# First rows of tile 0 loaded in two transfers and multiplied in four pieces, the last wide store issued by ScalarE, and a new plan of the whole order

## The chip, the cores and the metric

The kernel runs on one core of a Trainium2 chip. The metric is the time of one execution on the device in microseconds (us). Five engines work side by side, each through its own queue in order: TensorE (PE; its weight loads are listed as PEld), VectorE (DVE), ScalarE (ACT), GpSimd (POOL) and SyncE (SP), which issues the DMA transfers. They wait for each other on semaphores.

## What is computed

```python
# x: (2, 4160, 192), weight_gen: (2, 4160, 8 heads, 7)
w = softmax(weight_gen, axis=-1)
a[b, s, h] = sum_k w[b, s, h, k] * x_pad[b, s + k, h]          # 7 rows back, 24 columns a head
xk, xr = mu_k * a + (1 - mu_k) * a_prev, mu_r * a + (1 - mu_r) * a_prev
v = sigmoid(xr @ w_r) * (relu(xk @ w_k) ** 2 @ w_v)            # 192 -> 1024 -> 192
h = relu(v @ w_in)                                              # 192 -> 1024
out = (h * sigmoid(conv3(h, conv_w))) @ w_out                   # 1024 -> 192
```

All data are float32. A float32 product is split on the chip into a high and a low part, so that each product is several TensorE passes; the weights are split in the same way, once, at the start.

## The kernel before

The sequence of each batch is cut into ten tiles, `SIZES` = 238, 238, seven of 476, and 352 columns. For a tile i and a batch b the kernel loads rows of x (`rows`), multiplies them by the softmax weights `sw` into `prod` (seven products of 192 columns for a token slot), and sums the seven (`tok`). For tile 0 and for the slots named in `SUMS` TensorE adds them with an identity matrix and ScalarE copies the sum out; for all other slots GpSimd makes three additions. `mixing` turns tokens into columns and makes `xA` and `xB`. The first network (`moe1`: banks `pa`, sums in the banks `am` and `ar`, its split activations in `s`) and the second (`moe2`: banks `pc`, activations `h` and `g`, sums in the banks `bm` and `br`) each run over eight chunks of 128 of the 1024 columns. `store` empties `bm` and `br` and writes 128 wide and 64 narrow output rows (wide from `om` or `stage`, narrow from `att`).

In the first 70 us the weights come in too. `prepare` loads them through a ring of three buffers in `stage` and splits each chunk on ScalarE, VectorE and TensorE, with `bm` and `br` as places of work; in the names below `stage<-bm`, `pc<-stage` and `g<-stage,pc` are three VectorE steps of such a chunk. Twenty-six warming matmuls (`WARM`) that use only `signs` stand ahead of the real work on TensorE.

The order is not the one in which the code is written. Every operation is recorded with a wished time; `Program.schedule` then plans. A forward walk keeps a time for each engine, starts the ready operation of highest rank, and holds back two operations that share the SBUF port (`shares`: any GpSimd operation, and a VectorE operation with two operands in SBUF). A backward walk gives new ranks. After `ROUNDS` of the two, the operations are issued by their planned start (line 255, which is why every line of the profile says L255). `PACE` stretches the cost of every operation on an engine, `SLACK` is added where TensorE waits for that engine, and 3.507 us are added to each transfer. So a new number in these tables moves operations over the whole program, and the order that each engine executes is fixed when the kernel is built.

`attention` (line 569) holds `load` and `token`, `store` (line 971) holds `e0`, `e1` and `e2`.

Of the kernel before, what the change touches and what calls it, by code (L numbers as in the profile page):

```python
# [12 lines left out]
ALU = mybir.AluOpType  # L13
AX = mybir.AxisListType

NB, SEQ, DM, NH, KS, DFF = 2, 4160, 192, 8, 7, 1024
# [8 lines left out]
PART = [128] * NTILE  # L25
SLOTS = [2, 2] + [4] * 7 + [3]
EXTRA = [0] + [p * l - n for p, l, n in zip(PART, SLOTS, SIZES)][1:]
PAD = KS - 1
# [1 line left out]
NF = DFF // 128  # L30
LAG = 12
WARM = 26
SLACK = {"ACT": 0.311, "DVE": 0.274, "POOL": 0.239}
PACE = {"ACT": 1.045, "DVE": 1.035, "POOL": 1.037}
ROUNDS = 13
HELD = [85.0, 140.0, 215.0, 290.0, 365.0, 440.0, 515.0]
HIGH = range(5)
LOWS = {(NTILE - 1, NB - 1, k) for k in range(6, NF)}
SUMS = {(1, 0, 1), (1, 1, 0), (1, 1, 1)}
MODES = [0, 0, 0, 0, 0, 0, 2, 2, 2, 2, 2, 0, 2, 2, 2, 2, 2]  # L40

S_LAG, G_LAG = 3.25, 4.75
# [11 lines left out]
class Program:  # L54
# [81 lines left out]
    def schedule(self):  # L136
        n = len(self.ops)
# [46 lines left out]
        hold = ready  # L184
# [23 lines left out]
        def forward(rank):  # L208
            nonlocal when
            when = hold[:]  # L210
            start, last, table = [0.0] * n, 0.0, ACTF.Exp
            wires = dict.fromkeys(self.real, 0.0)

            def step(i, eng, t):
                nonlocal last, table
                start[i] = t
                if turns[i] is not None:
                    t = t + (0.0 if turns[i] == table else 1.3)
                    table = turns[i]
                end = t + late[i]  # L220
                if load[i]:
                    wires[eng] = max(wires[eng], t + dur[i] + 0.55) + moved[i]
                    end = wires[eng] + 3.507
                last = max(last, end)
                for j in succ[i]:
                    when[j] = max(when[j], t + dur[i] if eng in ("PE", "POOL") and eng == name[j] else end + slack(i, name[j]))
                return t

            walk((pred, succ), lambda i: (rank[i], i), step)
            return start, last  # L230

        def backward(start, last):
            nonlocal when
            full = [dur[i] + 0.55 + moved[i] + 3.507 if load[i] else late[i] for i in range(n)]
            when = [full[i] - dur[i] for i in range(n)]
            rank = [0.0] * n

# [32 lines left out]
def conv_moe_kernel(ctx: ExitStack, tc: tile.TileContext, xp, wg_first, wg_rest, w_k, w_v, w_r, w_in, conv_w, w_out, out):  # L270
# [116 lines left out]
    def at(t, fn, hold=0.0):  # L387
        plan.append((t, len(plan), fn, hold))
# [180 lines left out]
    def attention(i, b, t_load, t, dt_, eng, hold=(0.0, 0.0)):  # L569
        L = SLOTS[i]  # L570

        def load():
            rows_t[i, b] = rows_r()[:, :L + PAD]
            row = b * (SEQ + PAD) + STARTS[i] - EXTRA[i]
            SP.dma_start(out=rows_t[i, b], in_=bass.AP(tensor=xp.tensor, offset=xp.offset + row * DM, ap=[[L * DM, PART[i]], [1, (L + PAD) * DM]]))

        def token(l):
            if i not in tok_t:
                tok_t[i] = tok_r()
            p = prod_r()  # L580
            y = p.rearrange("p (k d) -> p k d", k=KS)
            w = sw[:, sum(slots[:i]) + b * L + l].unsqueeze(2).to_broadcast([128, KS, DM // NH, NH])
            eng.tensor_tensor(p.rearrange("p (k g h) -> p k g h", k=KS, h=NH),
                              rows_t[i, b][:, l:l + KS].rearrange("p k (g h) -> p k g h", h=NH), w, op=ALU.mult)
            if i < 1 or (i, b, l) in SUMS:

                def total():
# [17 lines left out]
            eng.tensor_tensor(tok_t[i][:, l, b * DM:b * DM + DM], y[:, 0], y[:, 1], op=ALU.add)  # L605

        at(t_load, load, hold[0])
        for l in range(L):
            at(t + l * dt_, lambda l=l: token(l), hold[1])

# [360 lines left out]
    def store(i, b, t):  # L971
# [11 lines left out]
        def e1():  # L983
            st["m"] = omt_r()
            ACT.activation(st["m"][:, :n], acc2["m"][:, :n], ACTF.Copy, scale=0.5)
            SP.dma_start(out=out[b, 0:128, t0 + a:t0 + n], in_=st["m"][:, a:n])

        def e2():
            DVE.scalar_tensor_tensor(out=st["b"][:, :n], in0=acc2["r"][0:64, :n], scalar=0.5, in1=st["b"][:, :n], op0=ALU.mult, op1=ALU.add)
# [158 lines left out]
```

## Time and profile before

| | us |
|---|---|
| median of 3 runs | 696.65 (696.64 to 696.85) |
| the profiled execution | 697.28 |
| span of its instructions, first to last | 695.5 |

| engine | busy us | share of the span | instructions |
|---|---|---|---|
| PE | 684.3 | 98% | 3473 |
| PEld | 603.6 | 87% | 3473 |
| ACT | 630.1 | 91% | 1333 |
| DVE | 589.9 | 85% | 1003 |
| POOL | 531.3 | 76% | 388 |

Matmuls are pipelined: a drawn matmul of 476 columns is 0.38 us long while the next one starts after some 0.22 us. So short stops of TensorE vanish in these pictures, and only what is longer than the overlap is shown as idle. A row of the timeline gives start, duration, engine, line, operation, output and input, the number of equal instructions merged, and in brackets the idle time of the engine before it with what ended it.

### The profile page before, as it was taken

The page shows a single profiled execution, that of the slowest core. Times are in us where ns is not written, and L with a number is a line of the kernel's source. Part 1 is how long each engine was busy: PE and PEld are TensorE (multiplying, and loading weights), DVE is VectorE, ACT ScalarE, POOL GpSimd, SP SyncE. Part 2 cuts the span into 40 slices and gives each one's busy share as a digit, 9 for nine tenths or more (in the row PEclk, how much of TensorE's full clock was granted, in tenths as well). Part 3 has the DMA queues.
Part 4 walks back from the last instruction along what each step waited for, and adds up shares of the span by engine and source line. Part 5 has one row for each costly group of instructions (what it writes and reads, how often), then busy time and mean ns, then how long its engine had stood idle before and what let it go on. Part 6 is the DMA issues. An engine that isn't in the chain of part 4 may idle for free.

```text
span 695.5 us, 10541 instructions
## 1 busy us (share of the span) xinstructions
PE 684.3 (98%) x3473; PEld 603.6 (87%) x3473; DVE 589.9 (85%) x1003; ACT 630.1 (91%) x1333; POOL 531.3 (76%) x388
## 2 busy tenths in 40 slices
PE   8999999999999999999999999999999999999997
PEld 7799887888888888888888888888888888899997
DVE  7999998889879898988798978988897768686787
ACT  4988899999999998999999899898999999999996
POOL 3899999996998699669976997599929996243335
PEclk9999999999999999999999999999999999999999
DMA  8987021222022321130222112121202000200011
GB/s 290 267 210 238 24 68 42 68 89 63 8 86 64 86 51 42 64 85 12 77 68 66 28 57 93 32 56 57 80 22 70 8 28 14 65 8 28 6 33 31
DMA packets 20791, 48.43 MB, mean 70 GB/s; under 512 B 3457, under 2 KB 16257, under 8 KB 20609
## 3 DMA queue, kind: packets, MB, share of 16 engines
q1 hardware_dynamic: 20736, 47.77, 23.6%
q8 instruction: 27, 0.44, 0.3%
q14 instruction: 28, 0.22, 0.1%
HBM read 27.40 MB, written 6.39 MB: 49 GB/s over the span
## 4 chain that ended last, share of the span: by engine, by line
PE 87%; DVE 6%; ACT 3%; DMA 2%; issue 1%; SPq 0%; DVEq 0%
PE pa L255 25%; PE pc L255 21%; PE bm L255 13%; PE am L255 12%; PE br L255 8%; PE ar L255 7%; DVE pc L255 2%; DMA wkB<-x 1%; DMA sw<-in_rest_dram 1%; DVE s L255 1%; ACT pc L255 1%; DVE g L255 1%; ACT pa L255 1%; DVE stage L255 1%; DVE mk L255 0%
## 5 line engine op out<-in xcount | busy, mean ns | idle before, releaser
L255 POOL TENSOR_TENSOR prod<-rows,sw 128x1344 f32<-128x1344 f32 x68 | 210.3, 3093 | 14.4 <-PE pa L255 11.6
L255 DVE SCALAR_TENSOR_TENSOR pc<-h,cw,pc 128x476 f32<-128x476 f32 (+1 forms) x276 | 193.6, 704 | 27.2 <-ACT pc L255 24.5
L255 ACT ACTIVATE pa<-pa 128x476 f32<-128x476 f32 (+2 forms) x280 | 151.9, 547 | 11.7 <-PE pa L255 9.2
L255 POOL TENSOR_TENSOR prod<-prod 128x576 f32<-128x576 f32 (+1 forms) x126 | 154.3, 1225 | 8.4
L255 PE MATMUL bm<-g,wo 128*128 128x476 f32 (+1 forms) x411 | 135.3, 376 | 0.4 <-ACT stage L255 0.4
L255 PE MATMUL am<-s,wv 128*128 128x476 f32 (+2 forms) x464 | 129.8, 357 | 0.0
L255 PE MATMUL pa<-xA,wkA 128*128 128x476 f32 (+2 forms) x438 | 112.0, 360 | 0.8 <-DVE s L255 0.8
L255 PE MATMUL pc<-x,wiA 128*128 128x478 f32 (+1 forms) x414 | 111.7, 375 | 0.4 <-ACT x L255 0.2
L255 DVE TENSOR_TENSOR s<-pa,s 128x476 fp32r<-128x476 f32 (+1 forms) x137 | 86.6, 633 | 19.5 <-ACT s L255 18.7
L255 PE MATMUL br<-g,wo 128*128 128x476 f32 (+1 forms) x274 | 100.6, 375 | 0.0
L255 PE MATMUL ar<-s,wv 128*128 128x476 f32 (+2 forms) x336 | 99.8, 350 | 0.0
L255 ACT ACTIVATE h<-pc 128x478 f32<-128x478 f32 (+1 forms) x138 | 78.3, 568 | 17.9 <-PE pc L255 16.6
L255 ACT ACTIVATE pc<-h,cw 128x476 f32<-128x476 f32 (+1 forms) x138 | 91.7, 665 | 0.8
L255 ACT ACTIVATE pc<-pc 128x476 f32<-128x476 f32 (+1 forms) x152 | 84.3, 555 | 8.3 <-DVE pc L255 4.5
L255 POOL TENSOR_TENSOR g<-stage,g 128x476 fp32r<-128x476 f32 (+1 forms) x41 | 47.5, 1160 | 56.0 <-ACT g L255 44.1
L255 PEld LDWEIGHTS pa<-xA,wkA 128*128 128x128 f32 x438 | 79.0, 188 | 12.2 <-DVE s L255 1.3
L255 PEld LDWEIGHTS am<-s,wv 128*128 128x128 f32 x464 | 81.0, 188 | 9.3
L255 PEld LDWEIGHTS pc<-x,wiA 128*128 128x128 f32 x414 | 76.3, 188 | 11.7 <-DVE g L255 1.0
L255 PEld LDWEIGHTS bm<-g,wo 128*128 128x128 f32 x411 | 76.5, 188 | 11.1 <-ACT stage L255 0.8
L255 PE MATMUL pa<-xB,wkB 128*128 128x476 f32 (+2 forms) x292 | 82.7, 359 | 0.0
L255 PE MATMUL pc<-x,wiB 128*128 128x478 f32 (+1 forms) x276 | 81.7, 376 | 0.0
L255 ACT CAST s<-pa 128x476 fp32r<-128x476 f32 (+1 forms) x137 | 76.4, 558 | 1.1
(170 smaller groups left out, 1178.2 us busy)
## 6 DMA issues: line engine op xcount, KB each, us to landing
rows<-in_x_dram SPq DMA_DIRECT2D x14, 960.0 KB, 5.0
xB<-rm SPq DMA_DIRECT2D x28, 119.0 KB, 2.3
rows<-in_x_dram SPq DMA_DIRECT2D x4, 768.0 KB, 6.6
xB<-mk SPq DMA_DIRECT2D x16, 119.0 KB, 2.3
rows<-in_x_dram SPq DMA_DIRECT2D x2, 864.0 KB, 5.3
r<-r SPq DMA_DIRECT2D x14, 119.0 KB, 2.2
x<-x SPq DMA_DIRECT2D x14, 119.0 KB, 2.2
out_dram<-stage SPq DMA_DIRECT2D x7, 238.0 KB, 2.0
```

Source lines behind the costliest of these rows:

```text
L255: getattr(self.real[eng], method)(*a, **k)
```

## The change

Four things are edited. The load of tile 0, batch 0 becomes two transfers of four rows each, at their place in one queue. Its two products become four instructions: first those of the rows of the first transfer (part 0), then those of the second (part 1). The last wide store is issued from ScalarE's queue, right behind the activation that fills `om`, no longer from SP's. And the plan is made with other numbers: `PACE`, `SLACK`, `ROUNDS`, 2.668 us for a transfer's end, and another set `SUMS` (slot 1 of tile 1, batch 0 now goes through GpSimd's additions, slot 3 of tile 2, batch 0 through TensorE).

```diff
-SLACK = {"ACT": 0.311, "DVE": 0.274, "POOL": 0.239}
-PACE = {"ACT": 1.045, "DVE": 1.035, "POOL": 1.037}
-ROUNDS = 13
+SLACK = {"ACT": 0.101, "DVE": 0.164, "POOL": 0.427}
+PACE = {"ACT": 1.038, "DVE": 1.018, "POOL": 1.022}
+ROUNDS = 16
...
-SUMS = {(1, 0, 1), (1, 1, 0), (1, 1, 1)}
+SUMS = {(1, 1, 0), (1, 1, 1), (2, 0, 3)}
...
-                    end = wires[eng] + 3.507
+                    end = wires[eng] + 2.668
...
-            SP.dma_start(out=rows_t[i, b], in_=bass.AP(tensor=xp.tensor, offset=xp.offset + row * DM, ap=[[L * DM, PART[i]], [1, (L + PAD) * DM]]))
+            for p, q in ((0, 4), (4, L + PAD)) if (i, b) == (0, 0) else ((0, L + PAD),):
+                SP.dma_start(out=rows_t[i, b][:, p:q], in_=bass.AP(tensor=xp.tensor, offset=xp.offset + (row + p) * DM,
+                                                                   ap=[[L * DM, PART[i]], [1, (q - p) * DM]]))
...
-        def token(l):
+        def token(l, part=None):
...
+            k0, k1 = (0, KS) if part is None else ((0, 4 - l), (4 - l, KS))[part]
...
+            eng.tensor_tensor(y[:, k0:k1].rearrange("p k (g h) -> p k g h", h=NH),
+                              rows_t[i, b][:, l + k0:l + k1].rearrange("p k (g h) -> p k g h", h=NH), w, op=ALU.mult)
+            if part == 0:
+                return
...
+        if (i, b) == (0, 0):
+            for part in range(2):
+                for l in range(L):
+                    at(t + (2 * part + l) * 0.03, lambda l=l, part=part: token(l, part), hold[1])
+            return
...
-            SP.dma_start(out=out[b, 0:128, t0 + a:t0 + n], in_=st["m"][:, a:n])
+            (ACT if last and b == 1 else SP).dma_start(out=out[b, 0:128, t0 + a:t0 + n], in_=st["m"][:, a:n])
```

VectorE at the head of the program, from the products of tile 0 on, before the change (`sw` are the softmax weights, `am` its place of work, `prod_82` and `prod_83` the products of the two slots):

```order
L255 TENSOR_TENSOR prod_82<-rows_80,sw 128x1344
L255 TENSOR_TENSOR prod_83<-rows_80,sw 128x1344
L255 TENSOR_SCALAR stage<-bm 128x512
L255 TENSOR_SCALAR pc_114<-stage 128x512
L255 TENSOR_REDUCE am<-sw 128x32
L255 SCALAR_TENSOR_TENSOR g_76<-stage,pc_114 128x512
L255 TENSOR_SCALAR stage<-br 128x512
L255 TENSOR_TENSOR sw<-sw,am 128x224
```

The same stretch of VectorE's queue after the change:

```order
L255 TENSOR_TENSOR prod_82<-rows_80,sw 128x768
L255 TENSOR_TENSOR prod_82<-rows_80,sw 128x576
L255 TENSOR_SCALAR stage<-bm 128x512
L255 TENSOR_TENSOR prod_83<-rows_80,sw 128x576
L255 TENSOR_SCALAR pc_114<-stage 128x512
L255 TENSOR_TENSOR prod_83<-rows_80,sw 128x768
L255 SCALAR_TENSOR_TENSOR g_76<-stage,pc_114 128x512
L255 TENSOR_SCALAR stage<-br 128x512
L255 TENSOR_REDUCE am<-sw 128x32
L255 TENSOR_SCALAR pc_114<-stage 128x512
```

The chunk's steps now stand between the pieces of the products, and `g_76` and `stage<-br` stand ahead of the reduction `am<-sw`, behind which `g_76` stood before.

VectorE where tile 0's result `x2_0` is written and tile 2 is mixed (`stage<-stage,pa1` and `att0`), at 72 us of the profile, before:

```order
L255 TENSOR_TENSOR wo_70<-pc0_114,g2_78 128x2x64
L255 SCALAR_TENSOR_TENSOR x2_0_73<-am_116,x2_0_73 128x238
L255 SCALAR_TENSOR_TENSOR x2_0_73<-am_116,x2_0_73 64x238
L255 TENSOR_TENSOR s0_104<-pc1_115,s0_104 128x476
L255 TENSOR_TENSOR stage_75<-stage_75,pa1_113 128x476
L255 SCALAR_TENSOR_TENSOR stage_75<-stage_75,onemu_61,pa1_113 128x476 x2
L255 SCALAR_TENSOR_TENSOR pc0_114<-h0_108,cw_62,pc0_114 128x476 x2
L255 TENSOR_TENSOR s1_105<-pa0_112,s1_105 128x476
```

The same place after:

```order
L255 TENSOR_TENSOR wo_70<-pc0_114,g2_78 128x2x64
L255 TENSOR_TENSOR stage_75<-stage_75,pa1_113 128x476
L255 SCALAR_TENSOR_TENSOR x2_0_73<-am_116,x2_0_73 128x238
L255 SCALAR_TENSOR_TENSOR x2_0_73<-am_116,x2_0_73 64x238
L255 SCALAR_TENSOR_TENSOR stage_75<-stage_75,onemu_61,pa1_113 128x476 x2
L255 TENSOR_TENSOR s0_104<-pc1_115,s0_104 128x476
L255 SCALAR_TENSOR_TENSOR pc0_114<-h0_108,cw_62,pc0_114 128x476 x2
L255 TENSOR_TENSOR att0_86<-att0_86,pa1_113 64x476
L255 TENSOR_TENSOR s1_105<-pa0_112,s1_105 128x476
```

One step of the mixing now stands ahead of `x2_0`, and another (`att0`) ahead of `s1`.

TensorE where the first unit's sums in `bm` are finished (the last `bm<-g3`) and the next unit's begin (`bm<-g0`), at 113 to 117 us of the profile, before:

```order
L255 MATMUL bm_118<-g3_79,wo_70 128x476 x3
L255 MATMUL br_119<-g3_79,wo_70 128x476
L255 MATMUL am_116<-s3_107,wv_69 128x476
L255 MATMUL pa1_113<-xA00_92,wkA_65 128x476 x3
L255 MATMUL pa1_113<-xB01_97,wkB_66 128x476 x2
L255 MATMUL br_119<-g3_79,wo_70 128x476
L255 MATMUL ar_117<-s3_107,wv_69 128x476
L255 MATMUL bm_118<-g0_76,wo_70 128x476 x2
```

The same place after, from the last `bm<-g3` on:

```order
L255 MATMUL bm_118<-g3_79,wo_70 128x476
L255 MATMUL am_116<-s0_104,wv_69 128x476
L255 MATMUL pa0_112<-xA10_94,wrA_71 128x476 x3
L255 MATMUL pc0_114<-x2_1_74,wiA_67 128x478 x3
L255 MATMUL pc0_114<-x2_1_74,wiB_68 128x478 x2
L255 MATMUL pa0_112<-xB11_100,wrB_72 128x476 x2
L255 MATMUL am_116<-s0_104,wv_69 128x476
L255 MATMUL ar_117<-s0_104,wv_69 128x476
```

Before, nine matmuls stood between the last use of `bm` and its next; now there are 31 (the next `bm<-g0` comes 22 rows below the first row shown).

## Rows read from the trace of the kernel before

**Rows 1.** Windows: length, then busy us (instructions) of PE, PEld, DVE, ACT, POOL; clock.
```profile
10.00:80.00 70.00, 65.97 (x467) 59.59 (x466) 65.97 (x143) 59.63 (x154) 62.69 (x41) 1.00 0.73 210
80.00:120.00 40.00, 39.43 (x203) 33.16 (x202) 36.70 (x59) 37.38 (x78) 38.00 (x27) 1.00 0.18 54
120.00:680.00 560.00, 560.00 (x2701) 492.57 (x2701) 470.13 (x769) 520.63 (x1077) 422.56 (x306) 1.00 0.18 50
```
**Rows 2.** Timeline of PE in the dense stretch: start us, duration us.
```profile
140.35 0.81 PE L255 MATMUL pa<-xA,wkA 128*128 128x476 f32 x3
140.99 0.60 PE L255 MATMUL pa<-xB,wkB 128*128 128x476 f32 x2
```
**Rows 3.** Timeline of all engines at the end of the program.
```profile
690.99 0.47 PE L255 MATMUL bm<-s,wo 128*128 128x354 f32 x2
...
691.68 0.52 DVE L255 SCALAR_TENSOR_TENSOR att<-br,att 64x353 f32<-64x353 f32 x1 [1.17 <-ACT att L255]
692.17 0.34 SPq L255 DMA_DIRECT2D out_dram<-om  x1
692.60 0.49 SPq L255 DMA_DIRECT2D out_dram<-att  x1
```
**Rows 4.** Timeline of PE at the head.
```profile
7.01 0.88 PE L1080 MATMUL ar<-signs 128*128 128x256 f32 x6
7.74 3.16 PE L255 MATMUL pa<-prod,ident 128*128 128x192 f32 x18
...
12.81 0.50 PE L255 MATMUL bm<-g,signs 128*128 128x512 f32 x1 [0.72 <-DVE g L255]
```
**Rows 5.** Timeline of DVE at the head.
```profile
6.03 3.03 DVE L255 TENSOR_TENSOR prod<-rows,sw 128x1344 f32<-128x1344 f32 x2
8.98 0.68 DVE L255 TENSOR_SCALAR stage<-bm 128x512 uint32<-128x512 uint32 x1
9.70 0.69 DVE L255 TENSOR_SCALAR pc<-stage 128x512 uint32<-128x512 uint32 x1
11.59 0.57 DVE L255 TENSOR_REDUCE am<-sw 128x32 f32<-128x224 f32 x1 [1.20 <-DMA sw<-in_rest_dram]
12.07 0.68 DVE L255 SCALAR_TENSOR_TENSOR g<-stage,pc 128x512 fp32r<-128x512 uint32 x1
...
13.27 0.38 DVE L255 TENSOR_TENSOR sw<-sw,am 128x224 f32<-128x224 f32 x1
13.56 0.69 DVE L255 TENSOR_SCALAR pc<-stage 128x512 uint32<-128x512 uint32 x1
...
14.89 0.56 DVE L255 TENSOR_REDUCE am<-sw 128x32 f32<-128x224 f32 x1
```
**Rows 6.** Timeline of SP at the first load of rows.
```profile
1.19 0.42 SPq L255 DMA_DIRECT2D rows<-in_x_dram  x1
```
**Rows 7.** DMA issues of that moment: KB each, us to landing.
```profile
rows<-in_x_dram SPq DMA_DIRECT2D x1, 768.0 KB, 4.6
```
**Rows 8.** Timeline of ACT at the first chunk of weights.
```profile
7.54 0.64 ACT L255 ACTIVATE bm<-stage 128x512 f32<-128x512 f32 x1 [3.20 <-DMA stage<-in_moe_w_k_dram]
```
**Rows 9.** Timeline of DVE from 72 us on.
```profile
72.73 0.84 DVE L255 SCALAR_TENSOR_TENSOR x<-am,x 128x238 fp32r<-128x238 f32 x2 [0.55 <-ACT x L255]
73.60 0.66 DVE L255 TENSOR_TENSOR s<-pc,s 128x476 fp32r<-128x476 f32 x1
74.17 0.64 DVE L255 TENSOR_TENSOR stage<-stage,pa 128x476 f32<-128x476 f32 x1
```
**Rows 10.** Timeline of PE from 77 us on.
```profile
78.17 0.60 PE L255 MATMUL pa<-xA,wkA 128*128 128x238 f32 x3 [0.80 <-DVE s L255]
```
**Rows 11.** Timeline of PE from 115.5 us on.
```profile
116.49 0.69 PE L255 MATMUL bm<-g,wo 128*128 128x476 f32 x2 [0.36 <-ACT stage L255]
```
**Rows 12.** Waits of PEld from 80 to 120 us: total, times, longest.
```profile
PEld pc L255 <- DVE g L255: 1.0, 2, 0.5
```
**Rows 13.** Timeline of POOL from 10 us on.
```profile
10.34 3.04 POOL L255 TENSOR_TENSOR prod<-rows,sw 128x1344 f32<-128x1344 f32 x1 [8.99 <-PE pa L255]
```

More of the change, by code (lines that the diff above doesn't have):

```diff
@@ L233, in backward @@
             nonlocal when
-            full = [dur[i] + 0.55 + moved[i] + 3.507 if load[i] else late[i] for i in range(n)]
+            full = [dur[i] + 0.55 + moved[i] + 2.668 if load[i] else late[i] for i in range(n)]
             when = [full[i] - dur[i] for i in range(n)]
@@ L574, in load @@
             row = b * (SEQ + PAD) + STARTS[i] - EXTRA[i]
-            SP.dma_start(out=rows_t[i, b], in_=bass.AP(tensor=xp.tensor, offset=xp.offset + row * DM, ap=[[L * DM, PART[i]], [1, (L + PAD) * DM]]))
-        def token(l):
+            for p, q in ((0, 4), (4, L + PAD)) if (i, b) == (0, 0) else ((0, L + PAD),):
+                SP.dma_start(out=rows_t[i, b][:, p:q], in_=bass.AP(tensor=xp.tensor, offset=xp.offset + (row + p) * DM,
+                                                                   ap=[[L * DM, PART[i]], [1, (q - p) * DM]]))
+        prod = {}
+        def token(l, part=None):
             if i not in tok_t:
                 tok_t[i] = tok_r()
-            p = prod_r()
+            if part != 1:
+                prod[l] = prod_r()
+            p = prod[l]
+            k0, k1 = (0, KS) if part is None else ((0, 4 - l), (4 - l, KS))[part]
             y = p.rearrange("p (k d) -> p k d", k=KS)
-            w = sw[:, sum(slots[:i]) + b * L + l].unsqueeze(2).to_broadcast([128, KS, DM // NH, NH])
-            eng.tensor_tensor(p.rearrange("p (k g h) -> p k g h", k=KS, h=NH),
-                              rows_t[i, b][:, l:l + KS].rearrange("p k (g h) -> p k g h", h=NH), w, op=ALU.mult)
+            w = sw[:, sum(slots[:i]) + b * L + l, k0:k1].unsqueeze(2).to_broadcast([128, k1 - k0, DM // NH, NH])
+            eng.tensor_tensor(y[:, k0:k1].rearrange("p k (g h) -> p k g h", h=NH),
+                              rows_t[i, b][:, l + k0:l + k1].rearrange("p k (g h) -> p k g h", h=NH), w, op=ALU.mult)
+            if part == 0:
+                return
             if i < 1 or (i, b, l) in SUMS:
```

## The prediction

> **What bounds the kernel now.** I read the windows first, since an average over the program mixes a loaded head with a dense body. From 120 to 680 us TensorE (PE) is busy in 560.00 of 560 us, at a granted clock of 1.00 [rows 1]; the other engines are not. In that stretch a matmul of 476 columns starts every (140.99 − 140.35)/3 = 0.213 us [rows 2]. The change leaves the number of TensorE's products as it is (one slot of `SUMS` is swapped for another), so no plan can shorten those 560 us. What can be won is what PE loses ahead of 120 us and what lies outside its work: 4.03 us of drawn idle time from 10 to 80 us and 0.57 us from 80 to 120 us [rows 1], some 4.6 us together, then the 7.74 us before its first product [rows 4], and the tail after its last [rows 3]. The drawn idle time is too small a count: three matmuls drawn as one take 0.81 us, so one is drawn as 0.81 − 2 x 0.213 = 0.38 us, and each stop hides 0.38 − 0.21, some 0.16 us more.
>
> Second, who makes PE wait there. VectorE (DVE) is busy in 65.97 of the 70 us from 10 to 80 us, idle for as long as PE is, and the stops that I opened name its results [rows 4, 10, 12]. So up to about 80 us the time is set by a chain in which DVE is nearly always full: a step taken off DVE, or an idle hole of DVE filled, moves PE. ScalarE (ACT) with 59.63 us and GpSimd (POOL) with 62.69 us of 70 have more room [rows 1]. Third, the rows at the two ends.
>
> The sum is made against the profiled execution, 697.28 us (695.5 of span and 1.78 around it); the median, 696.65, lies 0.63 us below it.
>
> **The tail.** DVE fills `att` from 691.68 to 692.20, SP issues the store of `om` at 692.17 for 0.34 us, and only at 692.60 that of `att`, with 0.49 us [rows 3]. With `om` issued from ACT's queue, SP is free and takes `att` at about 692.22: 0.38 us earlier. ACT has nothing behind that issue. No ACT issue of a transfer is in this trace. If it costs 0.49 us, as the longer of the two in [rows 3], `om` is on its way at 692.66, still ahead of the 693.09 that `att` needed; if it starts later than SP's by as much as the gain, 0.38 us, nothing is left, and by more it is a loss. Bounds −0.38 and +0.2, I take **−0.38**, since the issue stands right behind ACT's own activation and needs no signal to another engine.
>
> **The start of PE.** The first rows now come as 2 x 384 KB. I expect no gain from that alone. The load is issued at 1.19 us and takes 4.6 us to land, 5.8 us [rows 6, 7], while DVE begins the products at 6.03 us [rows 5] and PE's warming matmuls, ahead of the first product in its queue, last until 7.74 us [rows 4]. The one extra issue on SP costs 0.42 us [rows 6]; the transfers behind it are limited by what is queued in the DMA engines by then, so it costs nothing as long as a backlog stands; without that cover the second chunk and all behind come 0.42 us later.
>
> **The head on DVE.** A product of 1344 elements takes 3.03/2 = 1.515 us; `sw<-sw,am`, of the same form with 224, 13.56 − 13.27 = 0.29 us. That makes 1.225/1120 = 1.094 ns an element and 0.045 us for an instruction, so 0.885 us for a piece of 768 and 0.675 us for one of 576, and the four 3.12 us, 0.09 us more than now [rows 5]. The other half of the rows lies behind the first 512 KB chunk of `w_k` in the queue, with the same bytes ahead of it as that chunk had, so it lands when that did, about 7.5 us [rows 8], and the chunk lands earlier by the time of 384 KB: 512 KB took 7.5 − 5.8 = 1.7 us, so 384 KB 1.3 us, and ACT's first step on it starts near 6.2 us. DVE then: piece to 6.92, wait to 7.55, piece to 8.23, `stage` (9.70 − 8.98 = 0.72 us) to 8.95, piece to 9.62, `pc` 0.72 us to 10.34, last piece to 11.23, and `g` starts at 11.23 us where it started at 12.07 [rows 5]. PE's stop before 12.81 [rows 4] ends some 0.85 us earlier. But the reduction that stood ahead of `g` now comes later: from `g` to the second reduction DVE took 14.89 − 12.07 = 2.82 us, and 12.07 − 11.59 = 0.48 us for the first, so it gets there at 11.23 + 3.30 = 14.53, not 14.89: −0.36 us [rows 5]. Bounds −0.36 (the whole is kept) and +0.1 (the 0.09 of the split, nothing kept); I take **−0.25**, as the second chunk, which DVE needs behind `g`, lands no earlier than before.
>
> **From there to 78 us.** At 72.73 DVE stood idle for 0.55 us, waiting for ACT's `x`, and a mixing step `stage<-stage,pa` followed [rows 9]. In the new order this step stands ahead of `x2_0` and fills the hole: −0.55. But `att0` now stands ahead of `s1`, and a step of 476 columns of this kind takes 74.17 − 73.60 = 0.57 us [rows 9]; PE waited for that `s` at 78.17 with 0.80 us of idle time [rows 10]. So −0.55 + 0.57 = +0.02, and with the head **−0.23** up to 78 us.
>
> **From 78 to 120 us.** The 0.57 us of `att0` are no more to be done. PE's weight loads stood still twice for DVE's `g`, 1.0 us together [rows 12]. Bounds 0 (the step has only moved inside a queue that stays full) and −1.0; I take half, **−0.5**, near the 0.57 us of the step. At 116.49 us PE waits 0.36 us for ACT to empty the sums of the first unit [rows 11]. Before, nine matmuls stood between the last use of `bm` and its next, 9 x 0.213 = 1.9 us; now 31 do, 6.6 us, so the stop falls away with the 0.16 us it hides: **−0.52**. What is late next there is nothing drawn: this is the last stop before 120 us.
>
> **SUMS.** Both slots cost PE seven products and ACT a copy out, now for tile 2 and no more for tile 1. POOL's three additions go the other way, 576, 384 and 192 elements, so 1152/1344 x 3.04 = 2.6 us at the pace of its products [rows 13], and due earlier than before. POOL waited 8.99 us at the start [rows 13] and is idle for 7.3 of the 70 us after it [rows 1]: I cost it at nothing. If that cover fails, tile 1's columns are up to 2.6 us late, less what PE finds to do in the other batch.
>
> **How the numbers follow.** −0.38 − 0.23 − 0.50 − 0.52 = −1.63: 695.65 us in a profile like that of before, and less 0.63 a median of about **695.0 us**. By the bounds, −0.38 to +0.2, −0.34 to +0.12, −1.0 to 0, −0.52 to 0, the forecast has its own range of 694.2 to 695.9.
>
> **Rivals.** *Given back.* A full DVE has the same work by 80 us whatever its order (two products in two more pieces, one `att0` ahead of time), and PE's waits move instead of going: only the tail is left, 696.65 − 0.38 = 696.3 us. For it speaks that DVE and PE are idle for the same 4.03 us [rows 1]; against it that the stop at 116.49 is ACT's [rows 11]. *More than I could follow.* Only two or three places were followed and the whole order is new. Of 4.6 us drawn, the forecast takes 1.25 with the head; two fifths of the other 3.4 would be −1.4: 693.6 us. *Slower: DVE is held by POOL.* DVE's last piece of a product has both inputs in SBUF, and by my sum it starts at 10.34 us, where POOL starts its first product, 3.04 us long [rows 13]; before, DVE's products were done by 9.06 [rows 5]. If POOL is first and DVE has to wait for its end, DVE loses up to 3.04 us: 697.28 − 0.38 − 0.52 − 0.23 + 3.04 = 699.2, less 0.63 and with half of it made good in PE's later stops, 697.1 to 698.6; I take 698.3. What decides is whether DVE's last piece starts before POOL's product. No row here has two such instructions at once; the plan's rule (`shares`) keeps them apart in its own reckoning only. The Trainium skill, page "SBUF — State Buffer", section "Who interferes with whom", states that the two engines share a port pair under an exclusive lock: whichever issues first keeps it for its whole instruction, and a VectorE instruction with two SBUF inputs is then fully blocked by a GpSimd one that reads SBUF. No run here shows it yet; by that rule the rival's 3 us would be due whenever POOL starts first, and by the rows alone its price could be nothing. *It doesn't do what it says.* The second half of the rows lands later than 7.5 us, since 512 KB and it share the DMA engines; all of DVE from 7.55 us on is late by as much. By 0.85 us `g` starts no earlier than before, and the head's −0.25 and the 72 us place turn round: 696 to 697 us; the tail's gain stays.
>
> **Chances.** Forecast 0.47, given back 0.22, more 0.10, held by POOL 0.11, second half late 0.10. Under 0.2% (1.4 us, about what a measurement of this kernel can tell from no change) faster means below 695.25: all of the third, and about three quarters of the first: 0.46. Slower means above 698.05: most of the fourth, and of the last what is over 1.5 us late: 0.12. The rest, 0.42, is within. The range runs from 693.6 to 697.0 and leaves out the rival of POOL and the lower end of the third.
>
> **What would show it.** Right: SP's last issue near 0.05 us behind DVE's `att`; ACT's first step at 6.2, DVE's second piece at 7.5, its `g` near 11.2 and PE's first `bm<-g` before 12.1 us; no idle time of DVE ahead of `x2_0`; no stop of PE for `bm` at 113 to 120 us; PE's idle time from 10 to 120 us below 3.8. Wrong: POOL's first product beginning before DVE's last piece and that piece drawn or delayed by some 3 us; a store from ACT that ends last; new stops of PE on DVE or POOL between 20 and 80 us that make up the sum again; or a PE clock below 1.00 after the new stops.

## The result: slower by 0.6%, with a wide spread

The changed kernel takes 701.03 us (median of 11 runs, 698.28 to 706.01), the kernel before 697.12 us (11 runs, 696.46 to 697.47). The ratio is 1.006, with a 95% interval of 1.0045 to 1.0075. The forecast was 695.0 us, with a range up to 697.0. Not only the median moved: the runs of the kernel before lie within about 1 us, those of the changed kernel over almost 8 us. The profiled execution took 703.77 us, so its trace shows the trouble at more than its median size.

The windows of the changed kernel, as [rows 1] (length, then busy us of PE, PEld, DVE, ACT, POOL, PE clock, DMA share, GB/s):

```profile
10.00:80.00 70.00, 60.91 (x425) 55.47 (x424) 64.00 (x136) 53.33 (x140) 59.13 (x38) 0.98 0.71 211
80.00:120.00 40.00, 39.15 (x219) 33.91 (x219) 37.05 (x60) 37.97 (x79) 37.13 (x28) 1.00 0.16 46
120.00:680.00 560.00, 559.91 (x2687) 490.57 (x2686) 470.34 (x765) 521.94 (x1074) 423.02 (x303) 1.00 0.18 51
```

The body from 120 us on is as full as before. The loss is in the head: TensorE stands still for 9.09 of the 70 us from 10 to 80, where it was 4.03. Two stops make most of it. This is the view of TensorE's waits from 0 to 120 us (who is waited for: total us, times, longest), its first three rows:

```profile
PE bm L255 <- DVE g L255: 3.3, 2, 2.5
PE pc L255 <- DVE mk L255: 3.2, 1, 3.2
PE ar L1094 <- ACT signs L255: 2.6, 1, 2.6
```

The third stands at the start of both kernels. The longest wait of the first row, 2.47 us, is the stop that [rows 4] show with 0.72 us, and the kernel before has one wait for `mk`, of 0.6 us. Here is VectorE in the same stretch as [rows 5], then GpSimd and TensorE (start, duration, in brackets the idle time before and its releaser):

```profile
8.44 0.76 DVE L255 TENSOR_TENSOR prod<-rows,sw 128x576 f32<-128x576 f32 x1 [1.47 <-DMA rows<-in_x_dram]
...
10.38 0.69 DVE L255 TENSOR_SCALAR pc<-stage 128x512 uint32<-128x512 uint32 x1
10.97 3.46 DVE L255 TENSOR_TENSOR prod<-rows,sw 128x768 f32<-128x768 f32 x1
14.36 0.68 DVE L255 SCALAR_TENSOR_TENSOR g<-stage,pc 128x512 fp32r<-128x512 uint32 x1
```

```profile
10.58 3.04 POOL L255 TENSOR_TENSOR prod<-rows,sw 128x1344 f32<-128x1344 f32 x1 [9.23 <-PE pa L255]
```

```profile
15.09 0.50 PE L255 MATMUL bm<-g,signs 128*128 128x512 f32 x1 [2.47 <-DVE g L255]
```

VectorE's last piece, forecast at 0.885 us, is drawn 3.46 us long. GpSimd's product began 0.39 us ahead of it and ended at 10.58 + 3.04 = 13.62; the piece ends at 14.43, which is 0.81 us later. So it did its work after GpSimd's product, and the row of the held instruction counts the waiting as busy. `g` starts at 14.36 instead of 12.07 [rows 5]. This is the rival "DVE is held by POOL" of the prediction; below it is called the hold.

What it also does is seen on SP and on the DMA engines. The buffer of the first rows is free only when that piece ends, so the third load of rows is issued at 14.46 us, and behind it in SP's queue everything else. The kernel before, where VectorE's products were done by 9.06 us, and then the changed one:

```profile
9.09 0.33 SPq L255 DMA_DIRECT2D rows<-in_x_dram  x1
```

```profile
14.46 0.33 SPq L255 DMA_DIRECT2D rows<-in_x_dram  x1
```

The windows from 12.5 to 14.5 us, of the kernel before and then of the changed one, show the DMA engines at 0.78 and at 0.02 of their time:

```profile
12.50:14.50 2.00, 1.69 (x10) 1.65 (x11) 1.97 (x5) 0.88 (x2) 0.89 (x1) 1.00 0.78 282
```

```profile
12.50:14.50 2.00, 0.12 (x1) 0.00 (x0) 2.00 (x2) 0.00 (x0) 1.12 (x1) 1.00 0.02 6
```

The second stop comes at 55 us. Between 36 and 56 us a load of rows of 960 KB takes 10.6 us to land (6.6 in the kernel before) and the first chunk of `w_out` 10.1 us (DMA issues of the changed kernel):

```profile
rows<-in_x_dram SPq DMA_DIRECT2D x1, 960.0 KB, 10.6
stage<-in_moe_w_out_dram SPq DMA_DIRECT2D x1, 384.0 KB, 10.1
```

ScalarE works in order, so it stands still for that chunk, and the mixing step `att` behind it comes late, and with it what TensorE needs:

```profile
52.81 0.51 ACT L255 ACTIVATE bm<-stage 128x384 f32<-128x384 f32 x1 [2.55 <-DMA stage<-in_moe_w_out_dram]
53.26 0.44 ACT L255 ACTIVATE att<-pc,onemu 128x238 f32<-128x238 f32 x1
```

```profile
55.25 0.96 PE L255 MATMUL pc<-xA,wrA 128*128 128x238 f32 x3 [3.25 <-DVE mk L255]
```

```profile
56.00:58.00 2.00, 2.00 (x12) 2.00 (x10) 1.99 (x5) 2.00 (x6) 2.00 (x1) 0.50 0.38 84
```

The last row is the window from 56 to 58 us: after the stop of 3.25 us the granted clock is 0.50, that is 1.2 GHz. The thirteen matmuls of 238 columns from 55.25 to 58.14 us start 0.22 us apart, where those ahead of the stop start 0.11 us apart, so the stop cost some 1.4 us beyond itself.

The hold does not bring this second stop by itself. In the run warm_20 (below), with the same orders, the hold is there too and the same chunk is even issued 0.58 us later, at 43.29 us. It lands in 7.2 us, and ScalarE does not wait for it:

```profile
50.73 0.51 ACT L255 ACTIVATE bm<-stage 128x384 f32<-128x384 f32 x1
```

TensorE's wait for `mk` is then 0.6 us, as in the kernel before. So the trace of 703.77 us shows two things, the hold and a late landing, and why the transfers of that execution took so long stays open.

### The profile page after: what moved, and what is told of

Its sections match the earlier page's. It is cut to its first block, busy times and chain, and to the rows that moved or that the text cites. A ratio compares the mean times of both kernels' runs of the same rounds, so it can differ in the third digit from the quotient of the medians.

```text
span 702.0 us, 10563 instructions
## 1 busy us (share of the span) xinstructions
PE 685.5 (98%) x3473; PEld 604.8 (86%) x3473; DVE 593.7 (85%) x1005; ACT 632.3 (90%) x1333; POOL 531.6 (76%) x388
## 4 chain that ended last, share of the span: by engine, by line
PE 87%; DVE 8%; DMA 2%; ACT 2%; issue 1%; SPq 0%; DVEq 0%
PE pa L255 26%; PE pc L255 21%; PE bm L255 12%; PE am L255 12%; PE ar L255 8%; PE br L255 8%; DVE pc L255 2%; DMA stage<-in_moe_w_out_dram 1%; DMA rows<-in_x_dram 1%; DVE g L255 1%; DVE ar L255 1%; DVE s L255 1%; DVE stage L255 1%; DVE prod L255 1%; ACT pc L255 1%
## 5 line engine op out<-in xcount | busy, mean ns | idle before, releaser
L255 ACT ACTIVATE pa<-pa 128x476 f32<-128x476 f32 (+2 forms) x288 | 156.6, 547 | 15.5 <-PE pa L255 12.7
L255 PE MATMUL pa<-xA,wkA 128*128 128x476 f32 (+2 forms) x462 | 117.6, 357 | 1.0 <-DVE s L255 0.5
L255 DVE TENSOR_TENSOR s<-pa,s 128x476 fp32r<-128x476 f32 (+1 forms) x141 | 89.5, 635 | 15.2 <-ACT s L255 13.3
L255 PEld LDWEIGHTS pa<-xA,wkA 128*128 128x128 f32 x462 | 82.7, 189 | 12.9 <-DVE s L255 1.6
L255 PE MATMUL pa<-xB,wkB 128*128 128x476 f32 (+2 forms) x308 | 85.3, 355 | 0.0
L255 ACT ACTIVATE pc<-pc 128x476 f32<-128x476 f32 (+1 forms) x144 | 79.4, 551 | 5.2 <-DVE pc L255 4.2
L255 ACT CAST s<-pa 128x476 fp32r<-128x476 f32 (+1 forms) x141 | 78.7, 558 | 1.3
```

The lines of the kernel that those rows point to most:

```text
L255: getattr(self.real[eng], method)(*a, **k)
```

## The experiments

Each edit of an order was made on the finished order of the program: one instruction was taken out and put in elsewhere, all others kept their places. Where a number of the plan was changed, the program planned again. "Before" is 696.9 to 697.0 us in every comparison.

| run | median us | lowest to highest | ratio to before, 95% |
|---|---|---|---|
| after_again | 701.34 | 697.90 to 704.49 | 1.0042 to 1.0077 |
| piece_first | 698.46 | 697.76 to 702.28 | 1.0013 to 1.0038 |
| w_out_first | 698.96 | 697.85 to 706.88 | 1.0021 to 1.0067 |
| before_act_store | 696.78 | 696.23 to 699.31 | 0.9984 to 1.0011 |
| rows_late | 700.05 | 698.60 to 702.42 | 1.0039 to 1.0064 |
| piece_first_rows_late | 699.79 | 697.67 to 703.09 | 1.0024 to 1.0057 |
| no_split | 699.81 | 698.43 to 700.33 | 1.0027 to 1.0051 |
| old_numbers | 704.38 | 701.86 to 706.86 | 1.0080 to 1.0121 |
| landing_only | 699.67 | 699.07 to 701.91 | 1.0027 to 1.0050 |
| sums_only | 701.39 | 701.03 to 702.20 | 1.0038 to 1.0078 |
| paces_only | 703.61 | 701.30 to 704.10 | 1.0051 to 1.0109 |
| warm_32 | 699.04 | 698.32 to 700.64 | 1.0019 to 1.0043 |
| warm_20 | 702.01 | 699.22 to 704.01 | 1.0053 to 1.0088 |

**The changed kernel again.** No edit.

> The changed kernel once more, for its spread and for the trace of another execution. Both theories: the head is the same in every execution (VectorE's last product piece drawn at 3.0 to 3.5 us, `g` starting at 14.2 to 14.5 us). Theory 'transfers': the executions still lie between 698 and 706 us, and this trace, if it is of a shorter execution, has the same head but a shorter stop of TensorE near 55 us than the 3.25 us of the first trace. Rival 'one cause': the head alone differs between executions; then a shorter execution would have a shorter hold.

The spread is there again. The trace is of the slowest execution, 704.49 us; in its head the piece starts 0.20 us behind GpSimd's product and is drawn 3.64 us long, ending 0.82 us after GpSimd's. TensorE's wait for `mk` near 55 us is 3.3 us. So this run gave a second sight of both stops, but no short execution to compare.

**The piece ahead of its neighbour.** In VectorE's order:

```diff
 L255 TENSOR_TENSOR prod_83<-rows_80,sw 128x576
+L255 TENSOR_TENSOR prod_83<-rows_80,sw 128x768
 L255 TENSOR_SCALAR pc_114<-stage 128x512
-L255 TENSOR_TENSOR prod_83<-rows_80,sw 128x768
```

> One exchange of two VectorE neighbours in the changed kernel: the last product piece (768 elements) stands ahead of the step `pc<-stage`, so it can start near 10.4 us instead of 10.97, ahead of GpSimd's first product at 10.58 us. Theory 'hold' (whoever starts first keeps the other out): the piece takes 0.9 us instead of 3.46, GpSimd's product starts by 11.3 us or is drawn up to 0.7 us longer, `g` starts near 11.9 instead of 14.36, the third load of rows is issued near 11.3 instead of 14.46, and the median falls from 701.0 by 2.5 us or more; if the late loads behind it also make the stop at 55 us, to 696 to 697.5 us with a spread under 1.5 us. Rival 'the piece is slow by itself' (its input rows, its broadcast weights): it still takes about 3.4 us at its new place and the time stays at 701. Rival 'transfers are late for the new order's own sake': the head is repaired, but executions still reach up by 3 us or more above their fastest.

The two pieces are now drawn as one group of 1.61 us, `g` starts at 10.68, and TensorE has no idle time from 10 to 20 us:

```profile
8.43 1.61 DVE L255 TENSOR_TENSOR prod<-rows,sw 128x576 f32<-128x576 f32 x2
9.97 0.68 DVE L255 TENSOR_SCALAR pc<-stage 128x512 uint32<-128x512 uint32 x1
10.68 0.69 DVE L255 SCALAR_TENSOR_TENSOR g<-stage,pc 128x512 fp32r<-128x512 uint32 x1
```

The median falls by 2.9 us beside the changed kernel's 701.34 of the same comparison, and "the piece is slow by itself" falls. One reserve belongs to the trace: in this execution GpSimd starts only behind both pieces,

```profile
10.90 3.05 POOL L255 TENSOR_TENSOR prod<-rows,sw 128x1344 f32<-128x1344 f32 x1 [9.54 <-PE pa L255]
```

so it shows a head without a hold, not one that was saved from it. What shows the hold as a cause is the median of eleven executions, and with it the traces of the runs below. But the time stays 1.5 us above the kernel before, in its lowest run too, and the highest still reaches 702.28. So the expected 696 to 697.5 us was too good: the hold is not all. This kernel, with the hold off, shows what the new order itself does. These are the windows from 20 to 36, 36 to 60 and 60 to 80 us, of the kernel before:

```profile
20.00:36.00 16.00, 15.01 (x90) 12.71 (x89) 15.40 (x34) 14.70 (x43) 13.95 (x7) 1.00 0.89 266
36.00:60.00 24.00, 23.31 (x190) 22.42 (x189) 23.10 (x51) 20.68 (x53) 22.65 (x18) 1.00 0.81 202
60.00:80.00 20.00, 18.38 (x146) 16.93 (x145) 18.81 (x42) 17.50 (x42) 18.75 (x15) 1.00 0.38 143
```

and of this kernel:

```profile
20.00:36.00 16.00, 12.73 (x75) 10.10 (x74) 15.37 (x34) 13.85 (x42) 15.46 (x10) 1.00 0.91 259
36.00:60.00 24.00, 22.53 (x187) 21.86 (x186) 22.11 (x49) 21.08 (x54) 21.93 (x15) 1.00 0.79 193
60.00:80.00 20.00, 19.42 (x151) 18.33 (x150) 18.83 (x43) 16.73 (x41) 19.29 (x16) 1.00 0.41 149
```

From 60 to 80 us TensorE gains 1.04 us of busy time, from 20 to 36 it loses 2.28 us and from 36 to 60 us 0.78. With the gains from 10 to 20 us (0.72) and from 80 to 120 us (0.23) it stands still for 1.07 us more than in the kernel before, and the two profiled executions differ by 698.32 - 697.28 = 1.04 us. So these windows hold the whole of the difference. Its waits from 20 to 36 us name steps of the weights' chain and of the mixing:

```profile
PE br L255 <- ACT wv L255: 1.3, 2, 0.8
PE bm L255 <- DVE g L255: 0.8, 1, 0.8
PE br L255 <- DVE stage L255: 0.7, 1, 0.7
PE pa L255 <- DVE ar L255: 0.4, 1, 0.4
```

where the kernel before has 0.5 us for `g` and 0.3 us for a transfer in the same window. The same stops stand in the changed kernel's trace some 2.7 us later (0.80 and 0.58 us for `wv`, 0.79, 0.76 and 0.39 for the others), so they belong to the order and not to the exchange.

**The load of `w_out` ahead of one transfer.** In SP's order:

```diff
 L255 DMA rows_81<-in_x_dram 128x1920
-L255 DMA wiB<-x_1_74 64x2x512
 L255 DMA stage<-in_moe_w_out_dram 128x2x384
+L255 DMA wiB<-x_1_74 64x2x512
```

> The changed kernel with one exchange in SP's queue: the first chunk of `w_out` is issued ahead of the first `wiB` transfer, as in the kernel before, and the head is left as it is. Theory 'the order of the transfers makes the stop at 55 us': it lands some 1.7 us earlier (256 KB at the 155 GB/s that such transfers show) and the median falls by 1.5 us or more, to about 699 us. Rival 'all loads are late since the head, and this order hardly matters': no change beyond 1 us, median 700 to 702 us, with the same spread.

The median fits the first theory, but the lowest run is 697.85 and the highest 706.88, as wide as without the edit, and the trace (701.09 us) has the hold, 3.45 us, but not the stop at 55 us: the wait for `mk` is 0.6 us. With runs that fall to one side or the other of a race, twelve don't tell a small shift of the median. It is inconclusive by itself.

**The last store alone.** The kernel before, with one line of the change:

```diff
-            SP.dma_start(out=out[b, 0:128, t0 + a:t0 + n], in_=st["m"][:, a:n])
+            (ACT if last and b == 1 else SP).dma_start(out=out[b, 0:128, t0 + a:t0 + n], in_=st["m"][:, a:n])
```

> The kernel before with one part of the change alone: the last wide store is issued by ScalarE, every other instruction in its old place. Forecast of the prediction: -0.38 us, 696.7 us beside 697.1 of the kernel before. Rival 'the end is set by the transfers, not by their issue': `att` is issued 0.4 us earlier but the time falls by less than 0.2 us. Rival 'ScalarE's own queue of transfers is slower': no gain or a loss.

The end of the program in this kernel, as [rows 3]:

```profile
690.24 0.49 PE L255 MATMUL bm<-s,wo 128*128 128x354 f32 x2
...
690.93 0.52 DVE L255 SCALAR_TENSOR_TENSOR att<-br,att 64x353 f32<-64x353 f32 x1 [1.17 <-ACT att L255]
691.42 0.37 ACTq L255 DMA_DIRECT2D out_dram<-om  x1
691.48 0.49 SPq L255 DMA_DIRECT2D out_dram<-att  x1
```

`att` is issued 0.03 us after VectorE has filled it, where it waited 0.40 us before. From TensorE's last matmul (690.73) to the end of the span (694.4) it is 694.4 - 690.73 = 3.67 us, where it was 695.5 - 691.46 = 4.04: some 0.4 us less, as forecast (the spans are given to 0.1 us). In the time of whole runs, 0.14 us between the medians, this is below what the comparison can tell.

**The load of rows behind `w_out`.**

```diff
-L255 DMA rows_81<-in_x_dram 128x1920
 L255 DMA wiB<-x_1_74 64x2x512
 L255 DMA stage<-in_moe_w_out_dram 128x2x384
+L255 DMA rows_81<-in_x_dram 128x1920
```

> The changed kernel with one exchange in SP's queue: the 960 KB load of rows (batch 1 of tile 2, not used by GpSimd before about 60 us) is issued behind the first chunk of `w_out` and no longer ahead of it; the head with its hold stays. Theory 'a backlog of transfers ahead of w_out makes the stop at 55 us and the spread': that chunk lands by 47 instead of 52.8 us, TensorE's 3.25 us stop falls to under 1 us, and the executions gather at the lower end of the changed kernel: median 698 to 699 us, most within 1 us. Rival 'the hold in the head makes both, and the place of this load does not matter': median stays at 700.5 to 701.5 us, spread 698 to 704.

The long stop of TensorE is not in this trace (the wait for `mk` is 0.6 us), and ScalarE waits at the next small transfer instead:

```profile
52.37 0.19 ACT L255 ACTIVATE br<-stage 128x24 f32<-128x24 f32 x1 [0.88 <-DMA stage<-in_moe_conv_w_dram]
```

Still, the median hardly moves, and only the lowest of six executions, the profiled one, is at 698.6. Its head tells why it is the lowest:

```profile
9.88 0.95 DVE L255 TENSOR_TENSOR prod<-rows,sw 128x768 f32<-128x768 f32 x1
10.74 0.68 DVE L255 SCALAR_TENSOR_TENSOR g<-stage,pc 128x512 fp32r<-128x512 uint32 x1
```

```profile
10.01 6.75 POOL L255 TENSOR_TENSOR prod<-rows,sw 128x1344 f32<-128x1344 f32 x2 [8.65 <-DVE pc L255]
```

The order of VectorE is that of the changed kernel, and there is no hold: here the piece began 0.13 us ahead of GpSimd's product, and it is GpSimd that is late (two of its products last 6.1 us elsewhere, 6.75 here). So the same order of VectorE goes one way or the other from execution to execution. Six executions between 698.60 and 702.42 meet neither expectation (a median of 698 to 699, or of 700.5 to 701.5), so the theory that a backlog of transfers makes the spread is not borne out in the form in which it was put.

**Both edits together.** The diffs of piece_first and rows_late.

> Both exchanges together: VectorE's last product piece ahead of `pc<-stage`, and the load of rows behind the first chunk of `w_out`. Theory 'two causes, hold and backlog': the floor is that of the exchange in the head (697.8 us) and the upper executions (up to 702.3 with the head alone repaired) go: median 697.5 to 698.2 us, highest below 699.5. It does not come down to 696.9, the kernel before: what is left then belongs to the new order from 20 to 60 us. Rival 'hold and backlog are all': 696.5 us or less, as the prediction's sum without the hold.

No hold (GpSimd starts at 9.70 and its product is drawn 3.57 us, held for some 0.5 us by the piece that had just begun), and still 699.79 us: ScalarE waits 1.5 us for the conv weights. With `pc<-stage` still ahead of it the piece would have come at about 10.0 us, behind this start of GpSimd's, so here the exchange did save the head. Moving the rows takes the wait from one transfer to the other; it is no repair. Whether it is worse than the exchange alone (698.46) is not shown, since the two spreads overlap.

**The new numbers without the split, and the split with the old numbers.**

```diff
-            for p, q in ((0, 4), (4, L + PAD)) if (i, b) == (0, 0) else ((0, L + PAD),):
+            for p, q in ((0, L + PAD),):
...
-        if (i, b) == (0, 0):
-            for part in range(2):
-                for l in range(L):
-                    at(t + (2 * part + l) * 0.03, lambda l=l, part=part: token(l, part), hold[1])
-            return
```

> The new numbers of the plan and the ScalarE store, but tile 0's first rows in one transfer and two products; the plan is made anew by the program. If the split is what costs, through the collision in the head, this one is at 696 to 697 us with the spread of the kernel before. If the new numbers cost by themselves (less allowance for transfers and for VectorE), it lies at 697.5 us or above, with stops of TensorE on weights between 20 and 60 us. The forecast's view that the numbers give about 1.2 us back would have it at 695.5.

```diff
-SLACK = {"ACT": 0.101, "DVE": 0.164, "POOL": 0.427}
-PACE = {"ACT": 1.038, "DVE": 1.018, "POOL": 1.022}
-ROUNDS = 16
-SUMS = {(1, 1, 0), (1, 1, 1), (2, 0, 3)}
+SLACK = {"ACT": 0.311, "DVE": 0.274, "POOL": 0.239}
+PACE = {"ACT": 1.045, "DVE": 1.035, "POOL": 1.037}
+ROUNDS = 13
+SUMS = {(1, 0, 1), (1, 1, 0), (1, 1, 1)}
...
-                    end = wires[eng] + 2.668
+                    end = wires[eng] + 3.507
```

> The split load, the four pieces and the ScalarE store, with the numbers of the plan before (`PACE`, `SLACK`, `ROUNDS`, `SUMS`, 3.507 us); the plan is made anew by the program and its head differs (a chunk of weights stands ahead of the rows). If the new numbers are what costs, this one is near 696.5 us. If splitting costs by itself, through pieces of VectorE beside GpSimd's product, one piece is drawn at over 2 us and the time is 698 us or more.

Both are slower than the kernel before, by 2.9 and 7.5 us. So neither half of the change is the whole cause. Without the split there is no hold, and the time goes into other stops (1.3 us for `wkB`, 0.9 us for ScalarE's `g`). With the split and the old numbers the hold is back, at another time of the head:

```profile
12.68 3.66 DVE L255 TENSOR_TENSOR prod<-rows,sw 128x768 f32<-128x768 f32 x1
```

with GpSimd's product from 12.52 to 15.54 us. So in both plans that were made for the split, the last piece fell beside GpSimd's first product.

**One number at a time.** The kernel before with the ScalarE store, and in turn 2.668 us for 3.507, the new `SUMS`, and the new `PACE`, `SLACK` and `ROUNDS`.

```diff
-                    end = wires[eng] + 3.507
+                    end = wires[eng] + 2.668
```

> The kernel before with the ScalarE store and one number of the plan changed: 2.668 us for the end of a transfer instead of 3.507. Theory 'the smaller allowance for transfers is what costs': 698.5 us or more, with TensorE or ScalarE waiting for transfers ahead of 60 us, while the two kernels beside it stay within 1 us of 696.9. Theory 'any new order loses what the old one was chosen for': this and the two others each lose 0.5 us or more, at different places.

```diff
-SUMS = {(1, 0, 1), (1, 1, 0), (1, 1, 1)}
+SUMS = {(1, 1, 0), (1, 1, 1), (2, 0, 3)}
```

> The kernel before with the ScalarE store and the new set `SUMS` alone. Theory 'transfers': within 1 us of 696.9. Theory 'any new order': 0.5 us or more slower. If the swap of two slots itself were a burden (GpSimd's additions come due earlier), TensorE would wait for tile 1's columns (`xA`) between 20 and 40 us.

```diff
-SLACK = {"ACT": 0.311, "DVE": 0.274, "POOL": 0.239}
-PACE = {"ACT": 1.045, "DVE": 1.035, "POOL": 1.037}
-ROUNDS = 13
+SLACK = {"ACT": 0.101, "DVE": 0.164, "POOL": 0.427}
+PACE = {"ACT": 1.038, "DVE": 1.018, "POOL": 1.022}
+ROUNDS = 16
```

> The kernel before with the ScalarE store and the new `PACE`, `SLACK` and `ROUNDS` alone. Theory 'transfers': within 1 us of 696.9. Theory 'any new order': 0.5 us or more slower, by stops of TensorE on VectorE or ScalarE ahead of 120 us.

All three are slower, by 2.8, 4.5 and 6.7 us, and each loses at places of its own. The first two rows of TensorE's waits from 10 us on, of landing_only, then of sums_only, then of paces_only:

```profile
PE pa L255 <- DVE stage L255: 1.0, 2, 0.8
PE ar L255 <- ACT s L255: 0.6, 1, 0.6
```

```profile
PE bm L255 <- ACT g L255: 1.2, 2, 0.9
PE pa L255 <- DVE s L255: 1.1, 2, 0.9
```

```profile
PE ar L255 <- ACT s L255: 2.5, 1, 2.5
PE pa L255 <- ACT s L255: 1.7, 1, 1.7
```

"The allowance for transfers is what costs" falls, since the two kernels that keep 3.507 us lose more. What the three have in common is only that the order is another one. That this is the cause is argued: no edit here turns one of these orders back at the place where it loses.

**More and fewer warming matmuls.** The changed kernel, every order as it was:

```diff
-WARM = 26
+WARM = 32
```

> The changed kernel with 32 warming matmuls instead of 26 ahead of TensorE's first product; no instruction of any engine changes its place. TensorE starts about 1 us later, so GpSimd's first product, which waits for TensorE, starts near 11 us, behind VectorE's last piece at 9.9 to 11. Theory 'the spread of the changed kernel is a race of these two for the first start': TensorE is given more to do and yet the executions gather at the lower end, median 698.3 to 699.5 us, the piece drawn at 0.9 us, the upper values rare. Rival 'the spread is made by the transfers after 30 us': median 701 to 702 with the same spread of 6 us, since nothing about them is changed.

```diff
-WARM = 26
+WARM = 20
```

> The changed kernel with 20 warming matmuls instead of 26; every order as it was. TensorE starts about 1 us earlier, GpSimd's first product near 9.0 to 9.6 us, ahead of VectorE's last piece in every execution. Theory 'race': no execution at the low end is left (none under 699.5), the piece is drawn at 2.5 to 3.3 us, median 700.5 to 702.5. Rival 'transfers': the same distribution as with 26, from 698 on, or up to 1 us better for the earlier start.

GpSimd's first product waits for TensorE's reading of `prod`, so these matmuls move it against the piece, which waits for the rows. The two counts come out apart: with six more matmuls to do four of five executions take 699.54 us or less (median 699.04), with six fewer five of six take 701.55 or more (702.01). Beside the 22 executions with 26, half of them below and half above some 701.2 us, neither stands apart clearly. In the trace with 32 the piece starts at 10.49 us, GpSimd's product at 10.79, and the piece is drawn 0.95 us; in the trace with 20 these are 10.12, 9.73 and 3.45 us. That fits the race, turned by a count that touches nothing else; but it is one trace of each. TensorE's first product starts at 8.26 and 7.12 us in them, and with 26 warming matmuls it starts anywhere from 7.16 to 8.31 us in the traces with this plan. So what speaks for the race is the two sets of times more than the two traces. Two expectations were not met in full: one execution with 20 came in at 699.22, and the shift of TensorE's start is no larger than this scatter.

All traces of the changed kernel's head in one table, by the start of the two instructions:

| run (time of this execution) | GpSimd's product starts | VectorE's piece starts | piece drawn, us |
|---|---|---|---|
| changed kernel (703.77) | 10.58 | 10.97 | 3.46 |
| after_again (704.49) | 9.95 | 10.15 | 3.64 |
| w_out_first (701.09) | 9.97 | 10.37 | 3.45 |
| warm_20 (701.55) | 9.73 | 10.12 | 3.45 |
| rows_late (698.60) | 10.01 | 9.88 | 0.95 |
| warm_32 (699.04) | 10.79 | 10.49 | 0.95 |

Four executions with the hold take 701.1 us or more, two without it 699.0 or less. The 22 executions of the changed kernel without an edit fall apart in the same way: six take 697.90 to 698.79 us, sixteen 700.21 to 706.01, and none lies between. That the hold parts the two groups is likely, and not shown for the executions without a trace.

## Why the prediction was wrong, point by point

**The head.** The sum held that the pieces follow each other from 7.5 us and that the last one starts at 10.34 us and takes 0.885. The start was about right (9.88 to 10.97), and the step that failed is its duration: with GpSimd's product at 10.34 by the same sum, start against start was a tie. The prediction saw the tie, named the mechanism and gave it 0.11; between two engines whose starts move by some 1 us from execution to execution that was far too little, and by the two groups of times the hold may have come in sixteen executions of 22. The second half of the rows landed by 7.3 us in one trace and at 8.4 in another. The 8.4 of the changed kernel's own trace, 0.89 us behind the forecast 7.55, also meets the condition of the rival "it doesn't do what it says": by the prediction's sum it alone would have put `g` at 12.1 us. Where there was no hold the head gained about what was forecast: `g` started at 10.68 to 11.36 us in piece_first, rows_late and warm_32, beside the forecast 11.23 and 12.07 before.

The traces agree with the rule cited from the Trainium skill, "SBUF — State Buffer", section "Who interferes with whom": whoever issued first kept the other out for its whole instruction, in both directions (3.45 to 3.64 us for VectorE's piece, 0.5 us for GpSimd's product in piece_first_rows_late).

**The price of the hold.** The rival was given as 698.3 us, and the median came out at 701. Yet the hold itself was priced about right. Its sum stands on 697.28 − 0.38 − 0.52 − 0.23 − 0.63 = 695.5 us, so it took some 2.8 us for the hold; between the medians of the changed kernel and piece_first the hold is worth 2.9. What was wrong is the 695.5: without the hold the new order takes 698.46. What the price did not follow is that the piece also frees the buffer of the rows, so SP's queue and the DMA engines stood still with it (0.02 of their time from 12.5 to 14.5 us). The executions of 703.77 and 704.49 us have the stop at 55 us and the lower clock behind it on top, and those were in no term.

The miss adds up from medians: 701.03 − 695.0 = 6.0 us, of which the hold is 2.9, the loss of the new order without it 1.5 (698.46 − 696.92), and the gain of 1.63 that was forecast and did not come the rest.

**The places followed in the plan.** Seen in the changed kernel's trace, they came as described, and were given back beside it. VectorE and TensorE of the changed kernel, some 6 us later than in [rows 9, 10]:

```profile
78.36 0.64 DVE L255 TENSOR_TENSOR stage<-stage,pa 128x476 f32<-128x476 f32 x1
79.00 0.84 DVE L255 SCALAR_TENSOR_TENSOR x<-am,x 128x238 fp32r<-128x238 f32 x2
```

```profile
84.83 0.60 PE L255 MATMUL pa<-xA,wkA 128*128 128x238 f32 x3 [0.52 <-DVE s L255]
```

The mixing step fills VectorE's hole ahead of `x2_0`, and the wait for `s` behind `att0` is no longer than before, 0.52 us against 0.80 [rows 10]. Of the 1.04 us that piece_first gains from 60 to 80 us only some 0.5 is this place's (0.5 us for `s` instead of 0.80, and none for ScalarE's `x` instead of 0.2). The other 0.6 is a wait for `mk` that piece_first has between 36 and 60 us instead. Of the half of 1.0 us that was to go from 80 to 120 us [rows 12] nothing went: in piece_first the weight loads wait for `g` for 1.0 us again, in two stops. TensorE's idle time there is 0.34 us, 0.57 before [rows 1]. The stop at `bm` [rows 11] is gone, and a new one, for VectorE's `g`, stands close to it:

```profile
119.66 0.92 PE L255 MATMUL pc<-x,wiA 128*128 128x478 f32 x3 [0.33 <-DVE g L255]
```

With the 0.16 us that a stop hides this is 0.49 us, so the -0.52 was cancelled. What decided, apart from the hold, was the stretch that no term spoke of, 20 to 60 us, with 2.28 and 0.78 us lost. The second failed step is the one that summed three followed places and took the rest of the new order as neutral. The runs that plan anew with a part of the change point the same way: five of five lost 2.8 us or more beside the kernel before (old_numbers, which has the split, with a hold among its stops). The rival "given back" had the right mechanism but no price for the places that get worse.

**The tail.** -0.38 was forecast and some 0.4 measured in the span. It is the one term that held, and it is too small to be seen in the time.

**The other covers.** `SUMS` was costed at nothing; alone it makes a kernel of 701.39, but through a new order, so its own price is not known. The rows in two transfers did not start TensorE earlier, as forecast. A slip in the range changes nothing: by the four bounds as given the sum runs from 696.65 − 2.24 = 694.4 to 696.65 + 0.32 = 697.0 us, and not from 694.2 to 695.9.

**What stays open.** Which part of the stretch from 20 to 60 us would have to be put back was not tried. Nor is it known why the load of rows and the chunk of `w_out` landed so late in two traces, and why piece_first still has single executions up to 702.28; the kernel before has one at 701.29 among 34 as well. The mean granted clock of these two is 0.995 and 0.996, as in the changed kernel's two traces with the stop at 55 us (0.996 and 0.995). That they have such a stop too is not shown. No version was found that is measurably faster than the kernel before.

## What to carry to other kernels

When two engines share a port and the sum of your own rows puts their starts within half a microsecond, take the collision as a coin that is thrown in each execution, and go through all that waits for the loser: its results, its input buffers and the transfers queued behind those. Where a program plans its whole order from a few numbers, a new plan is a new draw: all five tried here lost. Following three places that get better says little, unless the places that could get worse are gone through as well. And where an execution time spreads, a harmless count ahead of the race (here warming matmuls) can turn it without a change to the suspects; it wants more executions than the five and six here, and the scatter of the start that it moves should be known.

## What the chip showed that was not expected

- A VectorE instruction that is kept out is drawn as busy: 3.45 to 3.66 us for 0.9 us of work. VectorE's busy share rose to 9.93 of 10 us in the worst stretch, which reads like a better use of it.
- The order of two starts 0.13 to 0.4 us apart decided over some 2.5 us in the head.
- After a stop of 2.47 us at 15 us the granted clock stayed at 1.00 (window 10 to 20 us); after one of 3.25 us at 55 us it was 0.50 for the window 56 to 58 us.
- One load order, one hold, two landings: the first chunk of `w_out` took 10.1 us in the changed kernel's trace and 7.2 us in warm_20's, and only the first made TensorE wait for 3.25 us.
- More work did not make a kernel slower: with 32 warming matmuls five executions had a median of 699.04 us, with 20 six had 702.01.
